# Fused attention and spatial gating on one core: fetches issued behind the last reader, separate buffers for the values' two readings, and a fixed start for the value parts

## The chip, the cores and the metric

The kernel runs on one core of a Trainium2 chip. The metric is the device time of one execution in microseconds (us). Two kernels are compared by the medians of their runs on the same chip. The profile is one execution, recorded by the hardware profiler; its times run from the first instruction.

## The reference

Attention in which neighbouring queries are averaged in twos, over 8 batches and 8 heads of 64, with 1152 keys and 576 pooled queries; its output goes through a gated unit with a spatial matrix over the 576 rows.

```python
def _attn_ref(q, k, v):                       # (8, 8, 1152, 64) each
    q_pool = q.reshape(B, H, S // 2, 2, D).mean(axis=3)
    scores = np.matmul(q_pool, k.transpose(0, 1, 3, 2)) / np.sqrt(D)
    scores = scores - np.max(scores, axis=-1, keepdims=True)
    attn = np.exp(scores)
    attn = attn / (np.sum(attn, axis=-1, keepdims=True) + 1e-09)
    return np.matmul(attn, v)

def _moe_ref(x, w_in, w_spatial, b_spatial, w_out):   # x: (8, 576, 512)
    h = np.maximum(x @ w_in, 0.0)
    u, v = h[..., :512], h[..., 512:]
    v_n = (v - v.mean(-1)) / np.sqrt(v.var(-1) + 1e-06)
    v_s = np.einsum('ts,bsd->btd', w_spatial, v_n) + b_spatial[None, :, None]
    return (u * v_s) @ w_out
```

## The kernel before

Numbers are float32, and matmuls take float16: each operand is scaled and split into a leading float16 part and a rest, and two or three products of parts stand for one product. The work is divided into 32 **pairs** (a batch and two heads); pair i belongs to batch i // 4. Four tasks belong to a pair, and each is a Python generator that issues a few instructions and then yields:

- `load_kq` (L218) fetches K and Q of a pair into one buffer `kq` (a single one for all pairs) in two transfers, L222 and L223, of 576 KB each. `prep` (L273) reads it: ScalarE squares of K and Q for a scale (L132 through L283, into a scratch part of `klo`), the sum over partitions on TensorE (L112) and the scale's exponent on VectorE (L117 to L122, `qkh`, `qks`, `qkr`), then the float16 parts: `xq` (L135), `qhi` (L138), scaled K (L302), its leading part `khi` (L304), its rest `klo` on GpSimd (L305), and nine copies between partitions, from L299 to L313, on the SyncE queue. Pair i + 2 is prepared while pair i is computed; there are three sets of these buffers.
- `norm_v` (L238) fetches the values of a pair (`load_v`, L226, 576 KB at L229 into `vt`, which has two buffers that the two tasks below take in turn) and squares them for the scale of the whole batch (L132 through L247). It runs four pairs ahead of the attention, because the scale of a batch needs its four pairs.
- `split_v` (L253) fetches the same values again and makes the leading part (L261, L262, on ScalarE) and the rest (L264, on GpSimd) in `vp`, one pair ahead.
- `maxima` (L317): 27 products with 384 keys on TensorE (L342, L333), each reduced on VectorE (L348), for the row maxima of the next pair; at its end they go as two rows into `xq` by a transfer (L363).

`attention` (L498) runs 18 steps of 128 keys for a pair: the scores' products (L506, L507) into one of three PSUM banks, the exponential on ScalarE (L512), a GpSimd subtraction that splits two tiles of probabilities (L524), and, four steps later, the values' products (L428, L432, L435). The generator yields 40 times, and at every such tick each of the pair's tasks is advanced at its own rate by `Pace` (L781): `Pace(gen, rate, at)` makes the first step when (ticks - at) x rate reaches 1. `values_ahead` (L267) chains norm_v of pair i + 4 and split_v of pair i + 1 at one rate of 0.35.

In pairs 0 to 7 the weights are converted from float64 (`load_weights`, L166) beside the attention, mostly on VectorE. After eight pairs a **gated unit** of two batches runs through the following eight, half a step per tick; the last one runs by itself at the end.

The order in which the engines do all this is not the order of the code. The framework schedules the recorded program: an instruction that is ready by its own estimate of times may be placed ahead of one that stands earlier in the code; the code's order counts as priority among those that are ready. Each engine then keeps the order that it was given, and waits in it.

Of the kernel before, what the change touches and what calls it, by code (L numbers as in the profile page):

```python
# [12 lines left out]
F32 = mybir.dt.float32  # L13
# [18 lines left out]
def attn_sgu_kernel(ctx: ExitStack, tc: tile.TileContext, qT, kT, v, w_in, w_spT, b_sp, w_out, out):  # L32
    nc = tc.nc
    P = 128
# [188 lines left out]
        nc.sync.dma_start(out=kq[:, KEYS:], in_=qT[b, hp].rearrange("h d r s -> (h d) (r s)"))  # L223
        state[i] = {"kq": kq}

    def load_v(i):  # L226
        b, hp = divmod(i, NHP)
        vt = ld.tile([P, 2, NC, D], F32, name="vt", bufs=2)
        nc.sync.dma_start(  # L229
            out=vt.rearrange("p h c d -> p h (c d)"),  # L230
            in_=v[b, 2 * hp : 2 * hp + 2].rearrange("h (p c) d -> p h (c d)", c=NC),
        )
        return vt

    vsq = {}
    vscale = {}

    def norm_v(i):  # L238

        b, hp = divmod(i, NHP)  # L240
        if hp == 0:
            vsq[b] = sm.tile([P, 2 * NHP], F32, name="vsq", bufs=2)
        vt = load_v(i)
        yield
        yield
        for h in range(2):
            square_sum(vsq[b][:, 2 * hp + h : 2 * hp + h + 1], vt[:, h], vt[:, h])  # L247
            yield
        if hp == NHP - 1:
            vscale[b] = yield from scale_of(vsq.pop(b), "v")  # L250
            yield

    def split_v(i):  # L253

        vt = load_v(i)
        yield
        yield
        s_v = vscale[i // NHP][0]
        vp = vps[i % 2]
        for h in range(2):  # L260
            nc.scalar.activation(vt[:, h], vt[:, h], AF.Copy, bias=0.0, scale=s_v)  # L261
            nc.scalar.activation(vp[:, h, :, D : 2 * D], vt[:, h], AF.Copy, bias=0.0, scale=1.0)  # L262
            yield
            nc.gpsimd.tensor_sub(vp[:, h, :, 0:D], vt[:, h], vp[:, h, :, D : 2 * D])  # L264
            yield

    def values_ahead(i):  # L267
        if i + NHP < NP:
            yield from norm_v(i + NHP)
        if i + 1 < NP:  # L270
            yield from split_v(i + 1)

    def prep(i):  # L273
        st = state[i]
        kq = st["kq"]
        X, KL, khh, qhl = (x[i % NSET] for x in (xq, klo, khi, qhi))
        k0 = kq[:, 0:KEYS].rearrange("p (c k) -> p c k", k=P)
        q0, q1 = kq[:, KEYS : KEYS + S], kq[:, KEYS + S :]
        st.update(qhl=qhl, khh=khh, X=X, KL=KL)

        sq = sm.tile([P, 2], F32, name="sq", bufs=2)
        for j in range(2):
            square_sum(sq[:, j : j + 1], kq[:, j * KEYS : (j + 1) * KEYS], KL[:, 0].rearrange("p c k -> p (c k)"))  # L283
            yield
        s, r = yield from scales(sq, "qk")
        esc = sm.tile([P, 1], F32, name="esc", bufs=NSET)
        nc.vector.scalar_tensor_tensor(
            out=esc, in0=r[:, 0:1], scalar=ESC, in1=r[:, 1:2], op0=ALU.mult, op1=ALU.mult
        )
        st["esc"] = esc  # L290
        s_k, s_q = s[:, 0:1], s[:, 1:2]
        nc.gpsimd.tensor_add(q0, q0, q1)
        yield

        lower, upper = slice(0, D), slice(D, P)
        head(X[:, 0], q0, s_q)
        rest(qhl[:, 1], q0, s_q, X[:, 0])
        yield
        nc.sync.dma_start(out=qhl[lower, 0], in_=X[lower, 0])  # L299
        nc.sync.dma_start(out=qhl[upper, 0], in_=qhl[lower, 1])  # L300
        for a, z in ((0, 5), (5, NC)):
            nc.scalar.activation(k0[:, a:z], k0[:, a:z], AF.Copy, bias=0.0, scale=s_k)  # L302
            yield
            nc.scalar.activation(khh[:, 1, a:z], k0[:, a:z], AF.Copy, bias=0.0, scale=1.0)  # L304
            nc.gpsimd.tensor_sub(KL[:, 0, a:z], k0[:, a:z], khh[:, 1, a:z])  # L305
            yield
        nc.sync.dma_start(out=khh[lower, 0], in_=khh[lower, 1])
        nc.sync.dma_start(out=khh[upper, 0], in_=khh[lower, 1])
        nc.sync.dma_start(out=qhl[lower, 1], in_=X[upper, 0])
        nc.sync.dma_start(out=khh[lower, 1], in_=khh[upper, 1])  # L310
        nc.sync.dma_start(out=X[lower, 1], in_=X[upper, 0])
        nc.sync.dma_start(out=KL[lower, 1], in_=KL[upper, 0])
        nc.sync.dma_start(out=KL[D:KR, 0], in_=KL[D:KR, 1])  # L313
        yield


# [54 lines left out]
    LAG = 4  # L371
    TAIL_SPLIT = 5
    TAIL_AT = 9
    PREP_AT = 3
    PREP_RATE = 0.35
    V_RATE = 0.35
    W_RATE = 0.25
    W_AT = 4
    MAX_RATE = 1.0
# [415 lines left out]
            gen = step(gen)  # L795

    load_kq(0)
    drain(norm_v(0))
    drain(prep(0))
    load_kq(1)  # L800
    for i in range(1, NHP):
        drain(norm_v(i))
    drain(maxima(0))
    drain(split_v(0))
    drain(prep(1))
# [1 line left out]
    spatial_weights = [None]  # L807
    credit = 0.0
    for i in range(NP):
        if i + 2 < NP:  # L810
            load_kq(i + 2)
        run = [
            Pace(maxima(i + 1), MAX_RATE) if i + 1 < NP else None,
            Pace(values_ahead(i), V_RATE),
            Pace(prep(i + 2), PREP_RATE, PREP_AT) if i + 2 < NP else None,
            Pace(weights, W_RATE, W_AT if i == 0 else 0),
        ]
        for _ in attention(i):
# [4 lines left out]
            while credit >= 1 and units:  # L823
                credit -= 1
                unit_step()
        for r in run[:3]:
            if r:
                drain(r.gen)
        weights = run[3].gen
        if ends_unit(i) and i < 2 * NHP:  # L830
            drain(weights)
            weights = None
# [50 lines left out]
```

## Time and profile before

| what | us |
| --- | --- |
| median of 3 runs (lowest, highest) | 1373.02 (1371.06, 1377.21) |
| profiled execution | 1378.83 |
| its span, first to last instruction | 1377.1 |
| first exponential (pair 0 begins) | 48.5 |
| pairs 0 to 7, with the weights' conversion | 280.1 |
| pair 31 and the last gated unit | 140.4 |
| TensorE / VectorE / ScalarE / GpSimd busy | 1222.1 / 967.1 / 970.6 / 847.0 |

In the rows of the profile PE is TensorE, PEld its weight load, DVE VectorE, ACT ScalarE, POOL GpSimd and SPq the queue of SyncE, which issues all transfers here. A row of a timeline has start, duration, engine, line, operation, out<-in; in brackets stands the idle time of the engine before it and what ended it. A row of waits has total, count and longest. A busy PE is not PE at its peak: matmuls are pipelined, and their ends are modelled.

### The profile page before, as it was taken

The numbers are of one execution on the slowest core, as the hardware profiler recorded it, in microseconds if no ns is written. First come the engines' busy times: TensorE is split into PE (matmuls) and PEld (weight loads), VectorE is DVE, ScalarE is ACT, GpSimd is POOL, SyncE is SP. The second block draws the span as 40 slices with busy tenths as digits, with TensorE's granted clock in tenths as the row PEclk, the third lists the DMA queues.
The fourth block names the chain that finished last, engine by engine and source line by source line (L and its number), as shares of the span: only waits on it lengthen the run. The fifth ranks groups of instructions, "written<-read, shape, count | busy, mean of one in ns | idle before, by whom it ended". The sixth has DMA issues, their size and how long they took to land.

```text
span 1377.1 us, 33478 instructions
## 1 busy us (share of the span) xinstructions
PE 1222.1 (89%) x13696; PEld 741.5 (54%) x13696; DVE 967.1 (70%) x2068; ACT 970.6 (70%) x1632; POOL 847.0 (62%) x492
## 2 busy tenths in 40 slices
PE   3677887788998999889998999889998999899998
PEld 1354555555554665556555666555555566556443
DVE  5799889986869767765668766775667866761455
ACT  6777678779966777768776886768776776655333
POOL 3587677878755666657774766667666576655000
PEclk9998899989999999999999999999999999999999
DMA  7533343434333231244332132244331131101002
GB/s 252 166 97 109 94 124 94 128 93 139 113 96 96 79 94 56 62 126 135 96 96 87 51 91 84 74 118 135 104 96 42 47 94 55 28 24 40 8 1 69
DMA packets 56346, 123.77 MB, mean 90 GB/s; under 512 B 8256, under 2 KB 16448, under 8 KB 56192
## 3 DMA queue, kind: packets, MB, share of 16 engines
q1 hardware_dynamic: 56192, 121.63, 29.8%
q8 instruction: 107, 1.75, 0.5%
q14 instruction: 47, 0.39, 0.1%
HBM read 83.56 MB, written 9.44 MB: 68 GB/s over the span
## 4 chain that ended last, share of the span: by engine, by line
PE 47%; DVE 25%; ACT 8%; POOL 7%; DMA 7%; issue 4%; SPq 1%; POOLq 0%; ACTq 0%; DVEq 0%
DVE mt L348 7%; PE pss L507 5%; PE pss L506 5%; PE pw L688 5%; POOL pt L524 4%; PE pm L342 4%; PE pw L731 4%; PE pw L646 3%; PE o L435 3%; PE o L428 3%; PE pw L582 3%; ACT pt L512 3%; DMA kq<-in_qT_dram 3%; PE o L432 3%; DVE vv L138 2%
## 5 line engine op out<-in xcount | busy, mean ns | idle before, releaser
L524 POOL TENSOR_TENSOR pt<-pt 128x1024 f16<-128x1024 f32 x288 | 567.8, 1977 | 265.9 <-ACT pt L512 253.8
L512 ACT ACTIVATE pt<-pss,lnp,esc 128x512 f32<-128x512 f32 x576 | 439.4, 776 | 156.7 <-PE pss L507 148.1
L348 DVE TENSOR_REDUCE mt<-pm 128x1 f32<-128x384 f32 x730 | 395.8, 552 | 139.1 <-PE pm L342 119.2
L435 PE MATMUL o<-vp,pt 128*128 128x65 f16 x2304 | 282.8, 198 | 20.2 <-POOL pt L524 19.9
L428 PE MATMUL o<-vp,pt 128*128 128x65 f16 x2304 | 284.8, 196 | 13.0 <-DVE xm L443 12.8
L506 PE MATMUL pss<-qhi,khi 128*128 128x64 f16 (+1 forms) x1152 | 279.6, 294 | 9.1 <-ACT pt L512 8.0
L432 PE MATMUL o<-vp,pt 128*128 128x64 f16 x2304 | 284.5, 196 | 0.0
L507 PE MATMUL pss<-xq,klo 66*128 66x64 f16 (+1 forms) x1152 | 280.6, 295 | 4.1 <-DMA xq<-mr 4.1
L428 PEld LDWEIGHTS <-pt 128*128 128x128 bf16 x2304 | 222.7, 101 | 85.1 <-DVE xm L443 22.0
L432 PEld LDWEIGHTS <-pt 128*128 128x128 bf16 x2304 | 221.6, 100 | 50.7 <-issue 10.5
L342 PE MATMUL pm<-khi,qhi 128*128 128x384 f16 x652 | 217.9, 335 | 32.6 <-DVE mt L348 27.7
L435 PEld LDWEIGHTS <-pt 128*128 128x128 f16 x2304 | 220.7, 100 | 31.6 <-POOL pt L524 24.8
L507 PEld LDWEIGHTS <-klo 66*128 66x128 f16 x1152 | 99.1, 100 | 48.8 <-issue 17.3
L132 ACT ACTIVATE klo<-kq 128x1152 f16<-128x1152 f32 x64 | 74.6, 1166 | 63.7 <-DMA kq<-in_kT_dram 49.4
L506 PEld LDWEIGHTS <-khi 128*128 128x128 f16 x1152 | 103.5, 100 | 27.9 <-issue 12.2
L342 PEld LDWEIGHTS <-qhi 128*128 128x128 f16 x768 | 76.8, 101 | 66.3 <-issue 28.5
L524 POOL TENSOR_TENSOR ptl<-ptl 128x1152 f16<-128x1152 f32 x32 | 71.1, 2221 | 57.9 <-ACT ptl L520 57.9
L305 POOL TENSOR_TENSOR klo<-kq,khi 128x640 f16<-128x640 f32 x64 | 85.1, 1341 | 20.1 <-ACT khi L304 19.8
L520 ACT ACTIVATE ptl<-pss,lnp,esc 128x256 f32<-128x256 f32 (+1 forms) x128 | 75.6, 591 | 24.8 <-PE pss L507 24.2
L264 POOL TENSOR_TENSOR vp<-vt,vp 128x576 f16<-128x576 f32 x64 | 80.6, 1264 | 20.3 <-ACT vp L262 20.3
L582 PE MATMUL pw<-wi_h,xg 128*128 128x512 f16 x240 | 90.1, 382 | 0.0
L731 PE MATMUL pw<-wo_h,vv 128*128 128x512 f16 x216 | 80.3, 381 | 4.7 <-DVE vv L138 4.7
(177 smaller groups left out, 2394.2 us busy)
## 6 DMA issues: line engine op xcount, KB each, us to landing
vt<-in_v_dram SPq DMA_DIRECT2D x64, 576.0 KB
kq<-in_kT_dram SPq DMA_DIRECT2D x32, 576.0 KB
kq<-in_qT_dram SPq DMA_DIRECT2D x32, 576.0 KB
khi<-khi SPq DMA_DIRECT2D x96, 144.0 KB
out_dram<-row SPq DMA_DIRECT2D x24, 256.0 KB
qhi<-xq SPq DMA_DIRECT2D x64, 72.0 KB
klo<-klo SPq DMA_DIRECT2D x32, 144.0 KB
vv<-in_w_in_dram SPq DMA_DIRECT2D x8, 512.0 KB
```

The source lines that it names most:

```text
L305: nc.gpsimd.tensor_sub(KL[:, 0, a:z], k0[:, a:z], khh[:, 1, a:z])
L342: nc.tensor.matmul(pm[:, :W], lhsT=qhl[:, h, c0 : c0 + P], rhs=khh[:, h, n * NB : (n + 1) * NB, :], start=True, stop=True,)
L348: nc.vector.reduce_max(out=mt[:, t, n : n + 1], in_=pm[:, :W], axis=AX.X)
L428: nc.tensor.matmul(o[:, t], lhsT=top[:, cols], rhs=vp[:, D : D + D1], start=c == 0 and t == 0, stop=False, skip_group_check=True,)
L432: nc.tensor.matmul(o[:, t, 0:D], lhsT=top[:, cols], rhs=vp[:, 0:D], start=False, stop=False, skip_group_check=True)
L435: nc.tensor.matmul(o[:, t], lhsT=rst[:, cols], rhs=vp[:, D : D + D1], start=False, stop=c == NC - 1, skip_group_check=True,)
L506: nc.tensor.matmul(o, lhsT=khh[:, h, c, :], rhs=qhl[:, h, q], start=True, stop=False)
L507: nc.tensor.matmul(o, lhsT=KL[0:KR, h, c, :], rhs=X[0:KR, h, q], start=False, stop=True)
L512: nc.scalar.activation(pt, ps, AF.Exp, bias=lnp, scale=esc)
L524: nc.gpsimd.tensor_sub(t.bitcast(F16)[:, :, 0::2], t, t.bitcast(BF16)[:, :, 1::2])
L582: nc.tensor.matmul(ph, lhsT=xa[:, cc, c0 : c0 + P], rhs=wa[:, cc, DH:DF], start=n == 0, stop=n == 3 * NCC - 1,)
L731: nc.tensor.matmul(py, lhsT=ga[:, fc, c0 : c0 + P], rhs=wa[:, fc, :], start=m == 0, stop=m == end - 1)
```

## The change

1. **K and Q**: `load_kq(i + 1)` is called at the end of `prep(i)`, behind the last copy, and no longer at the beginning of a pair's loop pass. PREP_AT goes from 3 to 2.
2. **Values**: the one name `vt` with two buffers becomes two names, `vn` for the squares and `vs` for the parts, with one buffer each; the fetch into a buffer is issued at the end of the task that has read it, for the next pair (`load_v(i + ahead, name)`).
3. **Rates**: norm_v and split_v are paced apart, norm_v at 0.4 from tick 0, split_v at 0.3 from tick 16 on.
4. **The start**: the squares of pairs 0 and 2 go through `vn`, those of 1 and 3 through `vs`, and the preparation of pair 0 stands ahead of the squares in the code.

The arithmetic is the same.

```diff
@@ -223,38 +223,40 @@
         nc.sync.dma_start(out=kq[:, KEYS:], in_=qT[b, hp].rearrange("h d r s -> (h d) (r s)"))
         state[i] = {"kq": kq}
 
-    def load_v(i):
-        b, hp = divmod(i, NHP)
-        vt = ld.tile([P, 2, NC, D], F32, name="vt", bufs=2)
-        nc.sync.dma_start(
-            out=vt.rearrange("p h c d -> p h (c d)"),
-            in_=v[b, 2 * hp : 2 * hp + 2].rearrange("h (p c) d -> p h (c d)", c=NC),
-        )
-        return vt
+    vts = {}
+
+    def load_v(i, name):
+
+        if i < NP:
+            b, hp = divmod(i, NHP)
+            vt = ld.tile([P, 2, NC, D], F32, name=name)
+            nc.sync.dma_start(
+                out=vt.rearrange("p h c d -> p h (c d)"),
+                in_=v[b, 2 * hp : 2 * hp + 2].rearrange("h (p c) d -> p h (c d)", c=NC),
+            )
+            vts[i, name] = vt
 
     vsq = {}
     vscale = {}
 
-    def norm_v(i):
+    def norm_v(i, name="vn", ahead=1):
 
         b, hp = divmod(i, NHP)
         if hp == 0:
             vsq[b] = sm.tile([P, 2 * NHP], F32, name="vsq", bufs=2)
-        vt = load_v(i)
-        yield
-        yield
+        vt = vts.pop((i, name))
         for h in range(2):
             square_sum(vsq[b][:, 2 * hp + h : 2 * hp + h + 1], vt[:, h], vt[:, h])
             yield
+        load_v(i + ahead, name)
+        yield
         if hp == NHP - 1:
             vscale[b] = yield from scale_of(vsq.pop(b), "v")
             yield
 
     def split_v(i):
 
-        vt = load_v(i)
-        yield
-        yield
+        vt = vts.pop((i, "vs"))
         s_v = vscale[i // NHP][0]
         vp = vps[i % 2]
         for h in range(2):
@@ -263,12 +265,8 @@
             yield
             nc.gpsimd.tensor_sub(vp[:, h, :, 0:D], vt[:, h], vp[:, h, :, D : 2 * D])
             yield
-
-    def values_ahead(i):
-        if i + NHP < NP:
-            yield from norm_v(i + NHP)
-        if i + 1 < NP:
-            yield from split_v(i + 1)
+        load_v(i + 1, "vs")
+        yield
 
     def prep(i):
         st = state[i]
@@ -311,6 +309,8 @@
         nc.sync.dma_start(out=X[lower, 1], in_=X[upper, 0])
         nc.sync.dma_start(out=KL[lower, 1], in_=KL[upper, 0])
         nc.sync.dma_start(out=KL[D:KR, 0], in_=KL[D:KR, 1])
+        if i + 1 < NP:
+            load_kq(i + 1)
         yield
 
 
@@ -371,9 +371,11 @@
     LAG = 4
     TAIL_SPLIT = 5
     TAIL_AT = 9
-    PREP_AT = 3
+    PREP_AT = 2
     PREP_RATE = 0.35
-    V_RATE = 0.35
+    NORM_RATE = 0.4
+    V_RATE = 0.3
+    V_AT = 16
     W_RATE = 0.25
     W_AT = 4
     MAX_RATE = 1.0
@@ -795,11 +797,13 @@
             gen = step(gen)
 
     load_kq(0)
-    drain(norm_v(0))
+    load_v(0, "vn")
+    load_v(1, "vs")
     drain(prep(0))
-    load_kq(1)
-    for i in range(1, NHP):
-        drain(norm_v(i))
+    drain(norm_v(0, "vn", 2))
+    drain(norm_v(1, "vs", 2))
+    drain(norm_v(2, "vn", 2))
+    drain(norm_v(3, "vs", -3))
     drain(maxima(0))
     drain(split_v(0))
     drain(prep(1))
@@ -807,11 +811,11 @@
     spatial_weights = [None]
     credit = 0.0
     for i in range(NP):
-        if i + 2 < NP:
-            load_kq(i + 2)
         run = [
             Pace(maxima(i + 1), MAX_RATE) if i + 1 < NP else None,
-            Pace(values_ahead(i), V_RATE),
+            Pace(norm_v(i + NHP), NORM_RATE) if i + NHP < NP else None,
+
+            Pace(split_v(i + 1), V_RATE, V_AT) if i + 1 < NP else None,
             Pace(prep(i + 2), PREP_RATE, PREP_AT) if i + 2 < NP else None,
             Pace(weights, W_RATE, W_AT if i == 0 else 0),
         ]
@@ -823,10 +827,10 @@
             while credit >= 1 and units:
                 credit -= 1
                 unit_step()
-        for r in run[:3]:
+        for r in run[:4]:
             if r:
                 drain(r.gen)
-        weights = run[3].gen
+        weights = run[4].gen
         if ends_unit(i) and i < 2 * NHP:
             drain(weights)
             weights = None
```

What the scheduler makes of this is seen in the orders. Line numbers of the changed kernel are lower by 2 in `prep` (L305 was L307, L310 was L312, L302 was L304), higher by 2 in `split_v` (L263 was L261) and from the attention on (L514 was L512, L522 was L520), and L229 has become L233.

**First place**: SyncE's queue, around the fetch of K and Q for pair 20, during pair 17. Before:

```order
L307 DMA khi_117<-khi_117 64x1152
L308 DMA khi_117<-khi_117 64x1152
L309 DMA qhi_120<-xq_114 64x576
L312 DMA klo_108<-klo_108 64x1152
L222 DMA kq<-in_kT_dram 128x1152
L310 DMA khi_117<-khi_117 64x1152
L313 DMA klo_108<-klo_108 2x1152
L223 DMA kq<-in_qT_dram 128x1152
L229 DMA vt<-in_v_dram 128x2x576
```

After:

```order
L305 DMA khi_117<-khi_117 64x1152
L306 DMA khi_117<-khi_117 64x1152
L310 DMA klo_108<-klo_108 64x1152
L222 DMA kq<-in_kT_dram 128x1152
L308 DMA khi_117<-khi_117 64x1152
L311 DMA klo_108<-klo_108 2x1152
L223 DMA kq<-in_qT_dram 128x1152
L363 DMA xq_113<-mr 1x9x128 x2
L233 DMA vs<-in_v_dram 128x2x576
```

K's fetch stands directly behind the copy of `klo` in both; the values' fetch has moved behind the row of the maxima.

**Second place**: ScalarE at the start, up to the first exponential (`pt`). `xq`, `kq` and `khi` belong to the preparation of pair 1, `vp_102` to the values of pair 1, `u` and `vv` to the weights. Before:

```order
L261 ACTIVATE vt<-vt,vs 128x576 x2
L262 ACTIVATE vp_102<-vt 128x9x64 x2
L135 ACTIVATE xq_114<-kq,qks 128x576
L302 ACTIVATE kq<-kq,qks 128x640
L302 ACTIVATE kq<-kq,qks 128x512
L304 ACTIVATE khi_117<-kq 128x640
L304 ACTIVATE khi_117<-kq 128x512
L132 ACTIVATE vv,wiq<-u 128x512
L150 ACTIVATE u<-vv 128x512
L132 ACTIVATE vt,vsq<-vt 128x576 x2
L157 ACTIVATE vv<-vv,bias_e 128x512
L512 ACTIVATE pt<-pss,lnp,esc 128x512 x2
```

After:

```order
L150 ACTIVATE u<-vv 128x512
L135 ACTIVATE xq_114<-kq,qks 128x576
L300 ACTIVATE kq<-kq,qks 128x640
L300 ACTIVATE kq<-kq,qks 128x512
L302 ACTIVATE khi_117<-kq 128x640
L302 ACTIVATE khi_117<-kq 128x512
L263 ACTIVATE vs<-vs 128x576 x2
L264 ACTIVATE vp_102<-vs 128x9x64 x2
L157 ACTIVATE vv<-vv,bias_e 128x512
L514 ACTIVATE pt<-pss,lnp,esc 128x512 x2
```

The split of pair 1's values has moved behind the preparation, and the weights' steps L132 and L150 and two squares have moved ahead of it.

**Third place**: ScalarE between the last exponentials of pair 11 and the first of pair 12; `vsq` marks the squares of values, `ptl` the exponentials of the last 64 queries. Before:

```order
L512 ACTIVATE pt<-pss,lnp,esc 128x512 x2
L261 ACTIVATE vt<-vt,vs 128x576
L512 ACTIVATE pt<-pss,lnp,esc 128x512
L261 ACTIVATE vt<-vt,vs 128x576
L512 ACTIVATE pt<-pss,lnp,esc 128x512
L520 ACTIVATE ptl<-pss,lnp,esc 128x5x64
L512 ACTIVATE pt<-pss,lnp,esc 128x512
L520 ACTIVATE ptl<-pss,lnp,esc 128x5x64
L512 ACTIVATE pt<-pss,lnp,esc 128x512
L132 ACTIVATE row,gsq<-u 128x576
```

After:

```order
L132 ACTIVATE vn,vsq<-vn 128x576
L514 ACTIVATE pt<-pss,lnp,esc 128x512
L132 ACTIVATE vn,vsq<-vn 128x576
L514 ACTIVATE pt<-pss,lnp,esc 128x512 x3
L132 ACTIVATE vn,vsq<-vn 128x576 x2
L522 ACTIVATE ptl<-pss,lnp,esc 128x5x64
L514 ACTIVATE pt<-pss,lnp,esc 128x512
L522 ACTIVATE ptl<-pss,lnp,esc 128x5x64
L132 ACTIVATE vn,vsq<-vn 128x576
L132 ACTIVATE row,gsq<-u 128x576
```

Two pairs' squares and the first half of a third's stand here now where none stood before, and a fetch of 576 KB lies between one pair's and the next's.

## The prediction

> **What bounds the kernel now.** I read the page's totals first, then the view by stages, then single pairs of heads side by side, then the waits.
>
> ```profile
> span 1377.1 us, 33478 instructions
> PE 1222.1 (89%) x13696; PEld 741.5 (54%) x13696; DVE 967.1 (70%) x2068; ACT 970.6 (70%) x1632; POOL 847.0 (62%) x492
> ...
> 0.00:48.50 48.50, 16.31 (x51) 5.90 (x52) 27.96 (x65) 30.95 (x62) 17.12 (x22) 1.00 0.71 226
> 48.50:328.60 280.10, 224.58 (x2803) 147.37 (x2803) 246.49 (x457) 215.70 (x364) 214.55 (x118) 0.90 0.37 109
> ```
>
> The columns of a stage are its length, then busy time of PE, PE's weight load, DVE, ACT and POOL, then the granted clock. Over the whole span PE is 89% busy. The start, 48.5 us until the first exponential, is a chain of fetches and small steps (PE 16.3 us busy). In the next 280.1 us, while the weights are converted, DVE is the fullest (246.5 of 280.1, PE 224.6). After that come the steady pairs:
>
> ```profile
> 405.00:451.30 46.30, 40.27 (x432) 24.26 (x430) 41.49 (x89) 31.95 (x55) 25.91 (x15) 0.93 0.25 74
> 451.30:490.00 38.70, 36.55 (x439) 23.05 (x438) 23.78 (x54) 30.62 (x53) 26.95 (x17) 1.00 0.29 86
> 490.00:530.10 40.10, 39.32 (x476) 24.29 (x474) 28.12 (x64) 28.98 (x51) 25.44 (x15) 1.00 0.29 83
> 530.10:568.60 38.50, 36.99 (x463) 22.59 (x461) 27.72 (x64) 26.91 (x48) 27.07 (x16) 1.00 0.30 86
> ...
> 845.70:885.00 39.30, 37.04 (x463) 22.61 (x461) 27.71 (x64) 26.82 (x47) 27.00 (x16) 1.00 0.28 84
> ...
> 1160.10:1199.30 39.20, 36.76 (x463) 22.44 (x461) 29.49 (x63) 23.54 (x39) 26.50 (x15) 1.00 0.11 25
> ```
>
> These are pairs 10 to 13, 21 and 29. In most of them PE is busy for 94 to 98% (39.32 of 40.10 in pair 12); pair 10, in which the gated unit normalises, is DVE's (41.49 of 46.30). ACT has about 10 us to spare in each.
>
> **The K and Q fetch.** What ACT waits for:
>
> ```profile
> ACT klo L132 <- DMA kq<-in_kT_dram: 49.4, 20, 4.7
> ACT klo L132 <- DMA kq<-in_qT_dram: 8.8, 12, 1.9
> ...
> 704.25 0.46 SPq L312 DMA_DIRECT2D klo<-klo  x1
> 704.77 0.88 SPq L222 DMA_DIRECT2D kq<-in_kT_dram  x1
> ...
> 707.93 0.38 SPq L223 DMA_DIRECT2D kq<-in_qT_dram  x1
> ...
> 710.01 1.16 ACT L132 ACTIVATE klo<-kq 128x1152 f16<-128x1152 f32 x1 [3.97 <-DMA kq<-in_kT_dram]
> ```
>
> ACT stands 49.4 + 8.8 = 58.2 us for these fetches. But the issue at 704.77 already comes 0.52 us after the L312 copy, which waits for the last reader of the buffer (the subtraction L305): the scheduler has hoisted it out of the next loop pass. The first order shown above has the same rows around it in the changed kernel: L222 directly behind the klo copy, then two copies, then L223. So **this edit gains 0 us**: the fetch is issued where it was. What hides the wait is PE's own work: pair 29 prepares no further pair and fetches no K, and takes 39.20 us against 39.30 of pair 21, which does. If that cover fails, the price is the one wait of PE at the end of that path:
>
> ```profile
> PE o L435 <- POOL pt L524: 19.9, 24, 2.3
> ```
>
> That is 19.9 us in the whole span, so I bound this edit by -10 (half of it gone) and +4. The +4: behind the last cast of a pair and ahead of the next K square 27 fewer short ACT operations stand now, over the last 21 pairs, so ACT waits 27 x 0.67 = 18 us longer there; a fifth of such waits reaching PE would be 4 us. PREP_AT moves the first step by one tick and is inside these bounds.
>
> **The start.** Now one buffer takes the values of pairs 1 and 3 for the squares and of pairs 0 and 1 for the splits in turn, so two fetches that stood one behind the other are serial with their readers.
>
> ```profile
> 29.22 0.37 SPq L229 DMA_DIRECT2D vt<-in_v_dram  x1
> ...
> 33.21 0.68 ACT L132 ACTIVATE vt<-vt 128x576 f32<-128x576 f32 x1 [0.17 <-DMA vt<-in_v_dram]
> ...
> 39.12 1.44 ACT L261 ACTIVATE vt<-vt,vs 128x576 f32<-128x576 f32 x2 [4.46 <-DMA vt<-in_v_dram]
> ...
> 39.62 0.15 DVE L122 TENSOR_SCALAR qkr<-qkh 128x2 int32<-128x2 int32 x1
> ...
> 41.21 2.43 POOL L264 TENSOR_TENSOR vp<-vt,vp 128x576 f16<-128x576 f32 x2 [6.23 <-ACT vp L262]
> ...
> 41.61 0.76 ACT L135 ACTIVATE xq<-kq,qks 128x576 f16<-128x576 f32 x1
> ...
> 43.30 1.06 PE L507 MATMUL pss<-xq,klo 66*128 66x512 f16 x3 [4.09 <-DMA xq<-mr]
> ...
> 44.75 0.61 ACT L132 ACTIVATE vv<-u 128x512 f32<-128x512 f32 x1
> ...
> 47.83 0.72 ACT L157 ACTIVATE vv<-vv,bias_e 128x512 int32<-128x512 int32 x1 [0.52 <-DVE vv L155]
> 48.46 1.43 ACT L512 ACTIVATE pt<-pss,lnp,esc 128x512 f32<-128x512 f32 x2
> ```
>
> A free fetch of values takes 33.21 - 29.22 = 4.0 us. Before, ACT stands until 39.12 for the values of split 1, splits them (2.5 us, to 41.61), prepares pair 1 (3.1 us, to 44.75), then does the weights' steps until 48.46. After, the second order above has the preparation ahead of split 1. Step by step: the squares of pair 3 still end near 29.1, the fetch for split 0 lands at 33.2, its parts end on POOL 43.64 - 39.12 = 4.5 us later, at 37.7; the fetch for split 1 lands at 37.9 + 4.0 = 41.9. Meanwhile the scales are there at 39.8, the preparation runs to 42.9, split 1 to 45.4, L157 takes 0.6, and the first exponential starts at 46.0 instead of 48.5: **-2.4 us**. The ends: not before its product (43.30 + 1.06 = 44.4, so -4.1); if the fetch meets other transfers and takes 6.8 us, as the one from 20.93 to 27.76 did, -0.6 at 47.9.
>
> ```profile
> 20.93 6.80 DMA vt<-in_v_dram
> ```
>
> **The squares of the values.** With a buffer of their own, their fetch waits only for squares, so the scheduler draws them forward: the 12 pairs of squares that stood beside pairs 14 to 25 now stand, with the four that belong there, between pair 9.9 and pair 13.6 (third order above). Costs:
>
> ```profile
> 641.55 0.69 ACT L132 ACTIVATE vt<-vt 128x576 f32<-128x576 f32 x1
> ...
> 642.89 0.78 ACT L512 ACTIVATE pt<-pss,lnp,esc 128x512 f32<-128x512 f32 x1
> 643.02 0.38 SPq L229 DMA_DIRECT2D vt<-in_v_dram  x1
> ...
> 647.00 1.44 ACT L261 ACTIVATE vt<-vt,vs 128x576 f32<-128x576 f32 x2 [0.36 <-DMA vt<-in_v_dram]
> ...
> 722.30:768.70 46.40, 40.69 (x432) 24.23 (x430) 41.14 (x89) 31.73 (x55) 25.07 (x14) 0.93 0.24 72
> ...
> 1038.20:1083.40 45.20, 38.84 (x432) 23.25 (x431) 41.47 (x89) 30.41 (x51) 24.93 (x14) 0.96 0.21 60
> ```
>
> Two squares take 642.89 - 641.55 = 1.34 us, so 12 x 1.34 = 16.1 us of ACT move into pairs 10 to 13. A new wait comes on top. A fetch lands 647.00 - 643.02 = 4.0 us after its issue, which the release precedes by some 0.4: 4.4 us. In the new order ten of these sixteen have only 1.2 to 3.6 us of ACT work since the squares before (three exponentials and nothing else in one case); the shortfalls add up to 18.4 us. Behind the waiting square on ACT stand the exponentials, and PE waits for those; on SP the row of the maxima (L363) and the copies of the next preparation stand behind a fetch that waits for its buffer. ACT was busy for 31.95 + 30.62 + 28.98 + 26.91 = 118.5 of 163.6 us there and waited some 8 us for K and Q, which leaves 37 us for 34.5 of new demand: it just fits, with nothing over. One direct comparison prices it: pair 18 (with one pair of squares) took 46.40, pair 26 (none, and else the same unit's step) 45.20, so 1.2 us in a normalising pair; elsewhere, where PE has no slack to lose, I take 0.1, the difference between pairs 21 and 29. 2.5 more in pair 10 and 9.5 in the others give 3 + 1 = **+4 us**; ends 0 (all in ACT's idle time) and +16 (34.5 less half of the 37, if half of the idle time lies where neither falls). Later the twelve are gone: 1.2 + 11 x 0.1 = **-2.3 us** (0 to -3.5).
>
> By the Trainium skill's page "SBUF — State Buffer", section "Summary: rules for kernel authors", such a fetch would be estimated with 358 GB/s, about 1.6 us for 576 KB; the row above shows 4.0, and the measurement decides. By the page the shortfalls would all but vanish and the +4 with them, and the sum would be near 1368.
>
> **The weights' stage.** There DVE's order changes (maxima of pairs 6 and 7 now stand ahead of the previous pair's divisions), with the same operations. Term 0. DVE idles 280.1 - 246.5 = 33.6 us there; a third of that either way, 11 us, is the bound.
>
> ```profile
> 8.99 0.16 DVE L287 SCALAR_TENSOR_TENSOR esc<-qkr 128x1 f32<-128x1 f32 x1
> ...
> L287 DVE SCALAR_TENSOR_TENSOR esc<-qkr 128x1 f32<-128x1 f32 x8 | 10.6, 1329 | 0.0
> ```
>
> A one-column DVE operation takes 0.16 us with POOL idle and 1.33 in this stage, so small shifts against POOL move DVE's time both ways. The same section of that page says that a DVE operation with two SBUF inputs and a GpSimd operation block each other fully; this row agrees, though it alone doesn't show the partner.
>
> **Sum.** -2.4 + 0 + 4 - 2.3 + 0 = -0.7 us against the profiled execution (span 1377.1, 1378.83 in all, so 1378.1). That execution lay 5.8 us above the median of the runs, 1373.02; on the runs' scale the forecast is **1372 us**.
>
> **Rivals.**
> 1. The fetch waits do go (the hoist differs on the chip): half of PE's 19.9 us, with the start, 1373 - 10 - 2.4 = about 1361. For it: 58.2 us of waits. Against: same rows in the order, and pair 29. Chance 0.08.
> 2. The weights' stage gains: 1373 - 11 - 1 = about 1361. For it: 33.6 us of DVE idle time and a new order; against: the operations are the same. Chance 0.20.
> 3. **Slower**: ACT becomes the bound in pairs 10 to 13. The waits there overlap no idle time of ACT, because that lies in other places. It decides once the waits and squares exceed 37 us, that is once a fetch takes over 4.6 us instead of 4.4 (ten fetches, 2.5 us left). Then 1373 - 2.4 - 2.3 + 16 = about 1384, and 1388 with the +4 of the K and Q fetch. Chance 0.22.
> 4. The edit doesn't do what it says: for K and Q that is my forecast.
>
> **How the numbers follow.** The forecast, within 0.5% (6.9 us, about what can be told from no change), has 0.46; the other 0.04 are split. Faster 0.08 + 0.20 + 0.02 = 0.30, same 0.46, slower 0.22 + 0.02 = 0.24. The range reaches from somewhat below rivals 1 and 2 to rival 3: 1358 to 1388.
>
> **What would show it.** In the changed profile: first exponential at 46 us (44.4 to 47.9); ACT's wait for K and Q still near 58 us, or more; a new wait of ACT squares for values' fetches, near 18 us, in pairs 10 to 13, and those pairs 4 us longer in sum; pairs 14 to 25 shorter by 2. If the K and Q wait falls below 30 us, or the weights' stage differs from 280 us by over 5, the prediction is wrong in that step.

## The result, and the profile after

The changed kernel takes 1410.88 us (median of 4 runs, 1407.43 to 1412.98) beside 1372.04 for the kernel before on the same chip: a ratio of 1.0275, 95% interval 1.0237 to 1.0313. It is 39 us slower by the medians. The forecast was 1372, its range 1358 to 1388. The profiled execution took 1412.54.

The totals of the changed kernel's page:

```profile
span 1410.8 us, 33474 instructions
PE 1231.4 (87%) x13696; PEld 745.1 (53%) x13696; DVE 983.3 (70%) x2068; ACT 972.4 (69%) x1632; POOL 851.0 (60%) x492
```

The same numbers of instructions keep DVE busy 16 us longer (967.1 before). Next the view by stages of the changed kernel: start, weights' stage, pairs 10 to 13, 18 to 25, 26 to 30, and pair 29 alone (columns as in the prediction):

```profile
0.00:47.40 47.40, 16.45 (x51) 5.80 (x52) 27.99 (x65) 31.09 (x62) 16.19 (x21) 1.00 0.72 230
47.40:320.00 272.60, 219.35 (x2787) 143.43 (x2787) 241.16 (x453) 215.79 (x361) 218.70 (x120) 0.92 0.37 113
...
401.80:578.50 176.70, 155.00 (x1786) 94.36 (x1784) 125.99 (x268) 132.11 (x251) 104.60 (x61) 0.97 0.37 112
...
731.90:1057.80 325.90, 297.87 (x3424) 182.56 (x3423) 223.56 (x486) 223.81 (x357) 209.20 (x121) 0.98 0.26 74
1057.80:1270.50 212.70, 190.56 (x2182) 116.69 (x2181) 153.74 (x322) 135.09 (x219) 125.38 (x71) 0.96 0.17 49
...
1190.50:1233.80 43.30, 38.68 (x463) 23.39 (x461) 31.68 (x63) 24.71 (x41) 26.95 (x15) 0.96 0.14 36
```

The three steady stages in the kernel before:

```profile
405.00:568.60 163.60, 153.13 (x1806) 94.19 (x1803) 121.11 (x269) 118.46 (x204) 105.36 (x61) 0.98 0.28 82
...
722.30:1038.20 315.90, 295.42 (x3424) 181.11 (x3422) 217.53 (x487) 233.35 (x389) 208.33 (x121) 0.98 0.31 92
1038.20:1236.70 198.50, 184.75 (x2182) 113.18 (x2180) 149.29 (x322) 134.24 (x218) 125.43 (x71) 0.98 0.17 49
```

The start gained 1.1 us and the weights' stage 7.5. Pairs 10 to 13 lost 13.1, 18 to 25 lost 10.0, 26 to 30 lost 14.2; with pairs 8 and 9 (81.8, before 76.4), pairs 8 to 30 lose 42 in all. Pair 29 reads no values for squares and fetches no K, and still goes from 39.2 to 43.3. The last square of values ends in pair 13 of the changed kernel. So something other than the value squares costs in pairs 18 to 30, where a gated unit runs beside the attention.

ScalarE's waits for fetches in the changed kernel (total, count, longest):

```profile
ACT klo L132 <- DMA kq<-in_kT_dram: 45.5, 17, 4.0
ACT klo L132 <- DMA kq<-in_qT_dram: 8.5, 9, 2.3
ACT vn L132 <- DMA vn<-in_v_dram: 7.9, 8, 1.8
```

K and Q: 54.0 us, near the 58.2 of before, as forecast. The squares' new wait is 7.9 us, not 18.

**Pair 29.** A piece of the changed kernel's timeline; `qhi` is the rest of Q, `u` the gated unit's product, `mt` a maximum:

```profile
1204.88 0.75 DVE L697 SCALAR_TENSOR_TENSOR row<-pw,r_v,b_bc 128x512 f32<-128x512 f32 x1
...
1205.55 1.16 DVE L138 SCALAR_TENSOR_TENSOR qhi<-kq,qks,xq 128x576 f16<-128x576 f32 x1
1206.05 2.41 POOL L526 TENSOR_TENSOR pt<-pt 128x1024 f16<-128x1024 f32 x1
...
1206.63 2.38 DVE L700 TENSOR_TENSOR u<-u,row 128x512 f32<-128x512 f32 x1
...
1208.93 0.54 DVE L348 TENSOR_REDUCE mt<-pm 128x1 f32<-128x384 f32 x1
...
1209.53 0.32 PE L342 MATMUL pm<-khi,qhi 128*128 128x384 f16 x1 [2.05 <-DVE mt L348]
```

The same place before:

```profile
1172.22 0.81 DVE L138 SCALAR_TENSOR_TENSOR qhi<-kq,qks,xq 128x576 f16<-128x576 f32 x1
...
1174.85 0.74 DVE L695 SCALAR_TENSOR_TENSOR row<-pw,r_v,b_bc 128x512 f32<-128x512 f32 x1
...
1175.50 0.55 DVE L348 TENSOR_REDUCE mt<-pm 128x1 f32<-128x384 f32 x1
1175.97 1.43 DVE L698 TENSOR_TENSOR u<-u,row 128x512 f32<-128x512 f32 x1
```

Before, the rest of Q is done ahead of the row, and a maximum stands between row and product. After, the rest of Q has slid between row and product, the product meets a GpSimd subtraction and ends only 0.55 us behind it (1209.01, 1208.46), and the maximum comes 4 us after the row. TensorE waits 2.05 us for it. An engine that is 70% busy on average sets the pace here, because beside a gated unit the program gives TensorE only two banks for the maxima.

### The profile page after: what moved, and what is told of

Its sections match the earlier page's. It is cut to its first block, busy times and chain, and to the rows that moved or that the text cites. A ratio compares the mean times of both kernels' runs of the same rounds, so it can differ in the third digit from the quotient of the medians.

```text
span 1410.8 us, 33474 instructions
## 1 busy us (share of the span) xinstructions
PE 1231.4 (87%) x13696; PEld 745.1 (53%) x13696; DVE 983.3 (70%) x2068; ACT 972.4 (69%) x1632; POOL 851.0 (60%) x492
## 4 chain that ended last, share of the span: by engine, by line
PE 42%; DVE 27%; ACT 9%; POOL 8%; DMA 7%; issue 5%; SPq 1%; POOLq 0%; DVEq 0%; ACTq 0%
DVE mt L348 8%; PE pss L508 5%; PE pss L509 5%; POOL pt L526 5%; PE pm L342 4%; PE pw L690 4%; PE pw L733 4%; PE pw L648 3%; ACT pt L514 3%; PE pw L584 3%; DMA kq<-in_kT_dram 3%; PE o L437 3%; PE o L430 2%; PE o L434 2%; DVE vv L138 2%
## 5 line engine op out<-in xcount | busy, mean ns | idle before, releaser
L514 ACT ACTIVATE pt<-pss,lnp,esc 128x512 f32<-128x512 f32 x576 | 440.9, 777 | 184.3 <-PE pss L509 180.0
L430 PE MATMUL o<-vp,pt 128*128 128x65 f16 x2304 | 285.5, 197 | 19.8 <-DVE xm L445 19.6
L508 PE MATMUL pss<-qhi,khi 128*128 128x64 f16 (+1 forms) x1152 | 280.1, 295 | 8.5 <-ACT pt L514 7.8
L437 PEld LDWEIGHTS <-pt 128*128 128x128 f16 x2304 | 221.3, 100 | 21.0 <-POOL pt L526 14.2
L132 ACT ACTIVATE klo<-kq 128x1152 f16<-128x1152 f32 x64 | 74.5, 1164 | 60.9 <-DMA kq<-in_kT_dram 45.5
L266 POOL TENSOR_TENSOR vp<-vs,vp 128x576 f16<-128x576 f32 x64 | 85.4, 1335 | 16.7 <-ACT vp L264 16.6
L522 ACT ACTIVATE ptl<-pss,lnp,esc 128x256 f32<-128x256 f32 (+1 forms) x128 | 75.6, 590 | 22.8 <-PE pss L509 22.5
L290 POOL TENSOR_TENSOR kq<-kq 128x576 f32<-128x576 f32 x32 | 47.2, 1476 | 72.9 <-ACT klo L132 58.8
```

The costliest lines, as they stand in the source:

```text
L430: nc.tensor.matmul(o[:, t], lhsT=top[:, cols], rhs=vp[:, D : D + D1], start=c == 0 and t == 0, stop=False, skip_group_check=True,)
L437: nc.tensor.matmul(o[:, t], lhsT=rst[:, cols], rhs=vp[:, D : D + D1], start=False, stop=c == NC - 1, skip_group_check=True,)
L508: nc.tensor.matmul(o, lhsT=khh[:, h, c, :], rhs=qhl[:, h, q], start=True, stop=False)
L514: nc.scalar.activation(pt, ps, AF.Exp, bias=lnp, scale=esc)
```

## The experiments

Each changed part was run alone and in pairs, then one cause after another was taken out. Ratios are to the kernel before on the same chip, with 95% intervals; a stage's time comes from one profile. Executions of one kernel differ by up to 14 us (run 14: 1354.35 to 1368.38). Pair 29, 39.2 or 39.1 in the kernel before and in runs 2, 3, 4 and 8, repeats to 0.1 us.

### Which part costs: runs 1 to 4

**Run 1**, on the kernel before:

```diff
-    PREP_AT = 3
+    PREP_AT = 2
```

> The kernel before with PREP_AT 2 in place of 3 and nothing else. Theory A (the preparation one tick earlier changes VectorE's order: one maximum fewer stands ahead of the scale steps, and the leading part of Q falls behind the gated unit's row and beside a GpSimd subtraction, so the maxima come late and PE waits): about +42 us over the 23 pairs from pair 8 to 30 and no gain at the start, 1400 to 1420 us. Theory B (the values: bunched squares and one buffer for each reading): no change, 1372 +- 5. Theory C (the place of the K and Q fetch): no change, 1372 +- 5.

Measured: 1390.11 us, 1.0132 (1.0092 to 1.0171). Theory A holds in kind but not in size: pairs 8 to 30 lost 25.6 us (pair 29: 43.1), and pairs 0 to 7 gained 13.2 (266.9).

**Run 2**, on the changed kernel:

```diff
-    PREP_AT = 2
+    PREP_AT = 3
-        if i + 1 < NP:
-            load_kq(i + 1)
...
     for i in range(NP):
+        if i + 2 < NP:
+            load_kq(i + 2)
```

> The changed kernel without its first part: PREP_AT 3 and the K and Q fetch at the beginning of a loop pass, but the values' two buffers, their rates, V_AT 16 and the new start. Theory A: the loss is gone and the start's 1 us and the weights' stage's 7 us stay, 1360 to 1372 us. Theory B: the loss stays, 1405 to 1415. Theory C: the loss is gone as under A.

Measured: 1387.89 us, 1.0124 (1.0071 to 1.0176). Theory A alone falls. Pairs 10 to 13 take 174.6 (before 163.6), the other steady stages are within 3 us, and pair 29 is at 39.2. The values cost too, at another place.

**Run 3**, the K and Q lines of the change alone on the kernel before:

```diff
+        if i + 1 < NP:
+            load_kq(i + 1)
...
-        if i + 2 < NP:
-            load_kq(i + 2)
```

> The kernel before with the K and Q fetch issued at the end of the preparation, PREP_AT 3. Theory A and B, and the prediction: 0 us, 1368 to 1376, with ScalarE's wait for K and Q still near 58 us. Theory C: 1405 to 1415.

Measured: 1373.58 us, 0.9999 (0.9980 to 1.0018). Nothing, as forecast; ScalarE's wait for K and Q is 61.9 us.

**Run 4**, the changed kernel with `PREP_AT = 3`:

> The changed kernel with PREP_AT 3 in place of 2. Theory A: the 42 us are gone, 1360 to 1372 us, and the leading part of Q stands ahead of the gated unit's row again in pair 29. Theory B: 1405 to 1415. Theory C: 1405 to 1415.

Measured: 1384.03 us, 1.0072 (1.0051 to 1.0094): the rest of Q stands ahead of the row again and pair 29 takes 39.2, but pairs 10 to 13 take 174.1. So there are two causes: PREP_AT, and the values.

### What the early step does: runs 5, 6, 13, 15, 16 and 17

**Run 5**, on run 1's kernel; `hold` is 4, the steps up to the scales, the next one follows at once, and all later steps of the preparation come one step sooner too:

```diff
                 self.gen = step(self.gen)
+                self.n += 1
+                if self.n == self.hold:
+                    self.sum += 1.0
```

> The kernel before with PREP_AT 2, as in the first run, and Q's leading part and rest taken one step (2.9 ticks) sooner behind the scales, so that in pairs 13, 21 and 29 VectorE's rest of Q (L138) stands ahead of the gated unit's row again, while the scales stay as early as in the first run. Theory A1 (that rest, behind the row, puts the unit's product against a GpSimd subtraction and the maxima come late): pairs 13, 21 and 29 go back to within 1 us of 38.5, 39.3 and 39.2 (from 41.7, 40.4 and 43.1), and the whole falls from 1390 to about 1380. Theory A2 (the scales themselves, one maximum earlier, and TensorE's sum for them): those pairs and the whole stay, 1390 +- 5.

Measured: 1394.49 us, 1.0156 (1.0124 to 1.0189). Pairs 13, 21 and 29 took 39.1, 39.2 and 39.5: the place of these steps, and not of the scales, is what cost there, as A1 has it. The whole did not fall: pairs 8 to 30 lost 14.9 instead of 25.6, but the weights' stage took 279.7 instead of 266.9.

**Run 6**, on the kernel before:

```diff
-            Pace(prep(i + 2), PREP_RATE, PREP_AT) if i + 2 < NP else None,
+            Pace(prep(i + 2), PREP_RATE, 2 if i < 2 * NHP else PREP_AT) if i + 2 < NP else None,
```

> The kernel before with PREP_AT 2 in pairs 0 to 7 and 3 behind them. In the first run pairs 0 to 7 took 266.9 us instead of 280.1, and pairs 8 to 30 lost 26. If both are the step's own doing, this has the gain without the loss: about 1361 us. Rival: pairs 0 to 7 differ between kernels by chance of their order (276.0 in the third run, whose edit has no work there), so that 1365 to 1375 comes out.

Measured: 1365.99 us, 0.9948 (0.9929 to 0.9967). Pairs 0 to 7 took 268.7, and pairs 8 to 30 are within 2 us of before. So the early step costs where a gated unit runs. That it pays elsewhere isn't shown: the rival (pairs 0 to 7 differ by chance of their order) expected 1365 to 1375 and holds as well. In the profiles of this study pairs 0 to 7 took 266.9 to 287.6 us with the early step there and 265.8 to 280.1 without it.

**Run 13**, on run 1's kernel: the row stays in PSUM, so the product reads one operand from there. The arithmetic is the same.

```diff
-                    out=gg[:, :n], in0=pz[:, :n], scalar=r_v, in1=b_bc[:, ba : ba + n], op0=ALU.mult, op1=ALU.add
+                    out=pz[:, :n], in0=pz[:, :n], scalar=r_v, in1=b_bc[:, ba : ba + n], op0=ALU.mult, op1=ALU.add
                 )
-                nc.vector.tensor_mul(u[:, fc, a : a + n], u[:, fc, a : a + n], gg[:, :n])
+                nc.vector.tensor_mul(u[:, fc, a : a + n], u[:, fc, a : a + n], pz[:, :n])
```

> The first run's kernel (PREP_AT 2 alone), and the gated unit's product takes its second operand, the row, from PSUM, where the row is written in place. Theory A1 (the product is held up by GpSimd while it reads two operands from SBUF): it takes 0.7 us whether GpSimd works or not, pairs 13, 21 and 29 go from 41.7, 40.4 and 43.1 to within 1 us of 38.5, 39.3 and 39.2, and the whole from 1390 to about 1378. Theory A3 (the order of the maxima behind Q's rest is the loss, whatever the product takes): those pairs stay within 1 us of the first run's.

Measured: 1379.77 us, 1.0068 (1.0042 to 1.0093). The product in the view of lines, by shape (busy, mean in ns), in the changed kernel:

```profile
L700 DVE TENSOR_TENSOR u<-u,row 128x512 f32<-128x512 f32 x32 | 33.6, 1051 | 0.4
```

In the kernel before, and in run 13:

```profile
L698 DVE TENSOR_TENSOR u<-u,row 128x512 f32<-128x512 f32 x32 | 27.5, 858 | 0.4
```

```profile
L698 DVE TENSOR_TENSOR u<-u,pw 128x512 f32<-128x512 f32 x27 | 18.3, 678 | 0.0
```

And run 13's pair 29 by stage and at the place shown above:

```profile
1164.90:1202.30 37.40, 37.00 (x466) 22.79 (x464) 26.50 (x63) 23.46 (x39) 23.53 (x15) 1.00 0.11 26
```

```profile
1180.59 0.81 DVE L698 TENSOR_TENSOR u<-u,pw 128x512 f32<-128x512 f32 x2
1180.81 1.90 POOL L524 TENSOR_TENSOR pt<-pt 128x1024 f16<-128x1024 f32 x1
...
1181.32 1.02 DVE L348 TENSOR_REDUCE mt<-pm 128x1 f32<-128x384 f32 x2
...
1182.25 1.07 DVE L138 SCALAR_TENSOR_TENSOR qhi<-kq,qks,xq 128x576 f16<-128x576 f32 x1
```

A GpSimd subtraction starts in the middle of the products, and they don't notice: no 128x512 product takes over 0.68 us. Pairs 13, 21 and 29 take 39.2, 38.4 and 37.4. That is what A1 expects, but it doesn't rule out A3: in this kernel the rest of Q has moved on behind the product and two maxima, so the maxima are no longer behind it either. The rows of pair 29 above favour A1. The product takes 2.38 - 0.68 = 1.70 us longer there than a free one and the rest of Q 1.16 - 0.81 = 0.35 longer than before, together the 2.05 us of the wait; this is an estimate from these rows. The Trainium skill's page "SBUF — State Buffer", section "Who interferes with whom", says that a VectorE instruction with two SBUF inputs contends with a GpSimd instruction that reads SBUF, and that one with at most one such input, outside its 2-port modes, does not; the rows of the product agree.

**Runs 15 and 16**, the same edit on the kernel before and on the changed kernel:

> The kernel before with the product's operand from PSUM and nothing else. Collisions hidden in the old order: 1368 to 1376, pairs 13, 21 and 29 within 0.5 us. Collisions that cost even there: 1360 to 1367.

> The changed kernel with the product's operand from PSUM. Theory A1: pairs 13, 21 and 29 (44.1, 44.1 and 43.3) lose 3 to 4 us each and the whole comes to about 1395; theory A3: 1408 to 1414.

Measured: run 15 1365.50 us, 0.9957 (0.9941 to 0.9973), pair 29 36.6; run 16 1394.21 us, 1.0175 (1.0160 to 1.0190), pairs 13, 21 and 29 39.4, 38.6 and 37.5. The product's collisions cost some 6 us even in the old order, and 14 (by the ratios) to 17 (by the medians) in the changed kernel. So they make only 8 to 10 of the 39 us between the two kernels. With the product in PSUM on both sides, run 16 is still 2.2% slower than run 15, and its pairs 8 to 30 take 939.0 us beside 898.1, a loss about as large as the 42 us with the row in SBUF. Pairs 18, 26 and 27 even take longer than in the changed kernel (51.8, 51.6 and 45.3 beside 48.9, 49.8 and 42.0).

**Run 17**. What run 13 left lay in the pairs in which the unit normalises. TensorE's waits in pair 26 of the changed kernel:

```profile
PE o L430 <- DVE xm L445: 3.6, 1, 3.6
PE pm L112 <- DVE mt L348: 2.8, 1, 2.8
PE pm L342 <- DVE mt L348: 2.8, 3, 1.4
```

And of the kernel before:

```profile
PE pm L342 <- DVE mt L348: 4.0, 3, 2.2
PE o L428 <- DVE xm L443: 1.0, 1, 1.0
```

The preparation's sum (L112) stood behind a maximum for 2.8 us, and the values' products behind a division of VectorE (`xm`) for 3.6 us. On run 13's kernel:

```diff
-            Pace(prep(i + 2), PREP_RATE, PREP_AT) if i + 2 < NP else None,
+            Pace(prep(i + 2), PREP_RATE, 3 if i >= 8 and i % 8 == 2 else PREP_AT) if i + 2 < NP else None,
```

> The thirteenth run's kernel (PREP_AT 2, product from PSUM) with PREP_AT 3 in pairs 10, 18 and 26. If the early step is what costs there (its sum over partitions and its scales stand between the normalisation's steps on TensorE and VectorE): those pairs go from 50.4, 50.1 and 48.9 to within 1 us of 46.3, 46.4 and 45.2, and the whole from 1379.8 to 1366 to 1371. If it is a neighbour's doing (what the pair before leaves behind): less than half of the 11.5 us goes.

Measured: 1371.69 us, 0.9980 (0.9958 to 1.0002). Pairs 10, 18 and 26 took 46.7, 45.2 and 45.2: what they had lost was the step's doing. In pair 26 the two waits, 2.8 and 3.7 us in run 13, fall to 0.3 and 1.0. The rest of the early step's price stays open: beside run 15, which has the same product and the old step, pairs 8 to 30 of this run are still 12 us longer (910.2 beside 898.1, the most in pair 17, 41.1 beside 37.5), and what costs there was not tried.

### What the values cost: runs 7 and 8

A piece of run 2's timeline, in pair 13:

```profile
530.17 0.61 ACT L520 ACTIVATE ptl<-pss,lnp,esc 128x320 f32<-128x320 f32 x1
533.42 0.68 ACT L132 ACTIVATE vn<-vn 128x576 f32<-128x576 f32 x1 [2.64 <-DMA vn<-in_v_dram]
...
534.11 0.76 ACT L512 ACTIVATE pt<-pss,lnp,esc 128x512 f32<-128x512 f32 x1
```

And in pair 27, where ScalarE waits for the single buffer of the parts:

```profile
1115.84 0.77 ACT L263 ACTIVATE vs<-vs 128x576 f32<-128x576 f32 x1 [3.11 <-DMA vs<-in_v_dram]
...
1117.58 0.77 ACT L512 ACTIVATE pt<-pss,lnp,esc 128x512 f32<-128x512 f32 x1
```

In both places a fetch holds up the exponential that stands behind it on ScalarE (in pair 27 with two short steps of the gated unit in between).

**Run 7**, on run 2's kernel (pair 4's first fetch also stands behind the start's squares, to keep the turns):

```diff
-            vt = ld.tile([P, 2, NC, D], F32, name=name)
+            vt = ld.tile([P, 2, NC, D], F32, name="vt", bufs=2)
```

> The second run's kernel (values' part alone) with the two buffers shared in turn again (one name with two buffers), fetches still issued at the end of a task: squares of the values stand beside the pairs where they stood before, not drawn forward. Theory B1 (the loss of 11 us in pairs 10 to 13 is the squares drawn forward into them): pairs 10 to 13 go back to 163.6 +- 2 us from 174.6, the whole to 1370 to 1377. Theory B2 (the loss is the split held back to tick 16, or the rates): pairs 10 to 13 stay near 174, the whole near 1388.

Measured: 1382.25 us, 1.0073 (1.0047 to 1.0099). Pairs 10 to 13 are back at 165.5, as B1 has it, but the whole is not: the last pairs of the batches, 15, 19, 23 and 27, took 2.6, 2.7, 3.6 and 3.7 us more than before. There the parts belong to the next batch, and they are held back to tick 16 in this run too. That this is what costs there was not tried by itself.

**Run 8**, on run 2's kernel:

```diff
-            vt = ld.tile([P, 2, NC, D], F32, name=name)
+            vt = ld.tile([P, 2, NC, D], F32, name=name, bufs=2 if name == "vn" else 1)
```

> The second run's kernel with two buffers for the squares' values, so that ScalarE hardly waits for their fetch while the squares stay drawn forward (30 of 56 late ones into pairs 9 to 12). If the loss in pairs 10 to 13 is the wait for the fetch: those pairs go back to 163.6 +- 3. If it is the squares' own time on ScalarE and what they push back: they stay at 171 to 176 or go over, and the whole stays near 1388.

Measured: 1368.96 us, 0.9980 (0.9963 to 0.9998). ScalarE's wait for the squares fell from 10.2 to 1.0 us, and pairs 10 to 13 took 166.0. Seven of their squares moved on to pairs 8 and 9; over pairs 8 to 13, with nearly as many squares as in run 2 (36 beside 38, 14 before), 3.6 us of a loss of 10.1 are left. So most of it was the wait, and little the squares' own time. Of the 19 us between runs 2 and 8, some 10 came from the weights' stage (265.8).

### Both mended, and the best version: runs 9 to 12, 14 and 18

**Runs 9 to 12** put the edits of runs 6 and 8 into the changed kernel (9), into run 2's (10), and each alone into the changed kernel (run 6's: 11, run 8's: 12).

> The changed kernel with two mends: PREP_AT 2 only in pairs 0 to 7 and 3 behind them, and two buffers for the squares' values. If the loss is the step in the pairs with a gated unit plus ScalarE's wait for the values' fetch, nothing of the 38 us is left, and the gains of the sixth and eighth run (start 43.5, pairs 0 to 7 near 266 us) come on top: 1355 to 1366 us. If something else of the change costs time (the K and Q fetch beside the two, the split held back to tick 16), 1372 to 1385.

> As the ninth run, but with the K and Q fetch at the beginning of a loop pass as before. If the K and Q edit is worth nothing, as the third run showed beside the kernel before, this comes out within 0.4% of the ninth run; if it costs or gains something in company with the others, the two differ by more.

> The changed kernel with PREP_AT 2 only in pairs 0 to 7, one buffer for the squares as in the change. By theory A the 27 us between the changed kernel and the fourth run lie in pairs 8 to 30 and go: 1376 to 1386, with pairs 10 to 13 still near 174 us. By theory B, that the one buffer is most of it, over 1395.

> The changed kernel with two buffers for the squares' values and PREP_AT 2 throughout. If the wait for that fetch costs 9 to 11 us in pairs 10 to 13 beside the early step too, and up to 10 more come from the weights' stage as between the second and the eighth run: 1390 to 1402, with pairs 18 to 30 as long as in the changed kernel (538.5 us). If the two losses are one and the same stall: 1408 to 1414.

Measured:

| run | us | ratio (95%) | weights' stage | pairs 10-13 | pairs 18-30 |
| --- | --- | --- | --- | --- | --- |
| changed | 1410.88 | 1.0275 (1.0237, 1.0313) | 272.6 | 176.7 | 538.6 |
| 9 | 1390.61 | 1.0131 (1.0112, 1.0149) | 285.5 | 165.9 | 521.1 |
| 10 | 1375.95 | 1.0023 (1.0006, 1.0041) | 271.8 | 168.2 | 522.3 |
| 11 | 1378.82 | 1.0052 (1.0029, 1.0075) | 268.0 | 167.9 | 520.8 |
| 12 | 1417.34 | 1.0325 (1.0303, 1.0346) | 287.6 | 170.5 | 538.7 |

Runs 9 and 12 lie outside every range that was expected of their totals, and run 10 differs from run 9 by 1.1% instead of 0.4. In the steady stages PREP_AT out of the later pairs takes nearly 18 us off pairs 18 to 30, as expected; the second buffer takes 9 (run 8 against 2), 6 (run 12 against the change) and only 2 us (run 9 against 11) off pairs 10 to 13. Run 11 keeps the single buffer and still has 167.9 in pairs 10 to 13, with 8.7 us of the wait in them: how much of a wait reaches TensorE depends on where it falls. What broke the totals is the weights' stage: run 9 is 13.7 us longer there than run 10, from which it differs by the K and Q lines alone. The stage in run 8, the shortest, and in run 12, the longest:

```profile
43.50:309.30 265.80, 211.50 (x2770) 138.73 (x2769) 235.73 (x459) 218.69 (x371) 216.79 (x119) 0.94 0.40 120
```

```profile
43.10:330.70 287.60, 226.86 (x2802) 147.46 (x2802) 256.26 (x463) 221.62 (x377) 217.16 (x120) 0.89 0.37 113
```

VectorE is busy 20.5 us longer with nearly the same instructions, and the stage is 21.8 us longer. In all twenty profiles of this study its length less VectorE's busy time lies between 28 and 36 us. So this stage is VectorE's, and its time follows how long VectorE's operations take. That the extra time lies beside GpSimd can be counted in the profiles: for each operation and shape take the median of those executions that no GpSimd instruction overlaps. What the overlapped executions of the stage take above it adds up to 58 us in run 8 and 77 in run 12, which is 18 of the 20.5 us. By the same count pairs 8 to 30 hold 82 us before and 102 after the change, 68 and 85 with the product in PSUM (runs 15 and 16): the product is one of several operations that are held up. How much of this reaches TensorE, and which lines bring it about, was not tried.

**Run 14**, the edits of runs 6 and 13 together on the kernel before, and **run 18**, the same two on the changed kernel:

> The sixth run's kernel (PREP_AT 2 in pairs 0 to 7, 3 behind them) with the product's operand from PSUM. If collisions of the product cost TensorE time in the pairs with a gated unit even in the old order: 4 to 10 us below the sixth run, 1356 to 1362. If they are hidden there (TensorE is 94 to 98% busy in those pairs): 1364 to 1368.

> The changed kernel with PREP_AT 2 only in pairs 0 to 7 and the product from PSUM: what is left of the change is the K and Q fetch and the values' part, to be set beside the fourteenth run (1359.6). If the values' part costs what the second run showed (14 us beside the kernel before), 1370 to 1377; if its cost was itself collisions of the product, 1356 to 1364.

Measured: run 14 1359.63 us, 0.9923 (0.9901 to 0.9945), the fastest of all and below both kernels; run 18 1375.17 us, 1.0011 (0.9992 to 1.0029). What lies between them, 0.9%, is the values' part with the K and Q lines, so most of the values' cost (1.2% in run 2) is not a collision of the product.

## Why the prediction was wrong

1. **The step that failed** is the sentence in the K and Q part: PREP_AT "moves the first step by one tick and is inside these bounds" (-10 to +4). It got no price of its own; the bounds were made from ScalarE's waits for the fetches and one wait of TensorE behind them. The prediction also took pair 29 for one that prepares no further pair, and so for a measure of what a preparation costs; but the rest of Q in the rows above is pair 31's, and pair 29 lacks only the fetch of a next K and Q and the squares of values. What the constant moves is the sum L112 on TensorE and the scales on VectorE, one maximum earlier, and behind them the rest of Q. Alone it costs 1.3% (run 1); out of the later pairs of the changed kernel it gives back 2.2% (run 11 against the change). Of the 25.6 us that run 1 lost in pairs 8 to 30, some 12 belong to the pairs that normalise (run 17 against run 13); a further part lies at the product in pairs 13, 21 and 29; 12 us are left open (run 17 against run 15). One part of the price stands in the prediction: it names operations that GpSimd holds up, with 0.16 and 1.33 us, but only for the weights' stage, with "small shifts". The pairs with a gated unit have such an operation too, in the chain that TensorE waits on.
2. **The value squares**: the mechanism was right, the size was not. The term +4 (0 to +16) measured +11.0 in pairs 10 to 13 with the values alone (run 2). The first half of rival 3 is what happened in this part, the waits overlap no idle time of ScalarE: run 8 takes the wait away, and the 11 us shrink to 2.4 (in pairs 8 to 13, 10.1 to 3.6). The condition it named, waits and squares above 37 us, did not hold: in these pairs of the changed kernel the wait was at most 7.9 us, and ScalarE was busy 13.7 us longer (132.1 beside 118.5). The waits were overestimated (18; 10.2 in run 2 and 7.9 in the changed kernel), and the share of them that reaches TensorE underestimated: the term took a tenth of a microsecond for a pair, from two pairs in which no square of the values waits. The 37 us of idle time answered how much ScalarE can do, not whether an exponential stands behind a wait.
3. **Later pairs 14 to 25**, -2.3: with the values alone 153.4 + 316.9 beside 153.7 + 315.9, so +0.7 (run 2). Their going gave nothing that can be seen.
4. **The start**, -2.4 (-0.6 to -4.1): the first exponential came at 47.4, -1.1.
5. **The weights' stage**, 0 within 11: 7.5 us shorter, inside the bound, but beyond the 5 us at which the prediction called this step wrong. Nearly the same operations took VectorE 5.3 us less (241.2 beside 246.5). The kernels of this study spread from 265.8 to 287.6, -14 to +8 of the kernel before.
6. **K and Q fetch**, 0: right beside the kernel before (run 3); beside the other edits it changes the weights' stage (runs 9 and 10).

The range ended at 1388, rival 3 with 4 us for the K and Q fetch. That run 2, the values alone, also comes to 1388 is luck, since its parts are others. The changed kernel is 27 us above run 4, which lacks the early step alone, and that step is what put it out of the range.

## What to carry to other kernels

A constant that moves one task by a tick is priced by the rows it changes on each engine in its order, and above all on those whose result a two-bank loop waits for. Where VectorE and GpSimd both work from SBUF, look for VectorE operations with two durations in the view of lines; an operand left in PSUM takes such an operation out of the collision (0.4% here). A wait moved to ScalarE is free only if no exponential stands behind it: count what is queued behind the wait, not the idle time of the engine.

## What the runs showed of the hardware

VectorE's 128x512 product with both operands in SBUF took 0.68 to 0.69 us free and up to 2.38 beside a GpSimd subtraction; with one operand in PSUM never more than 0.68. A one-input operation can be held up as well. In the changed kernel:

```profile
L121 DVE TENSOR_SCALAR qks<-qkh 128x2 int32<-128x2 int32 x32 | 17.9, 559 | 0.6
...
L121 DVE TENSOR_SCALAR vs<-vh 128x1 int32<-128x1 int32 x8 | 1.2, 152 | 0.2
```

The same line takes 559 ns on average with two columns (up to 2.08 us) and 152 with one (never over 0.16, though GpSimd works beside most of them). The maxima's reductions from PSUM take 0.52 to 0.56 us with and without GpSimd beside them. In pair 29 of the changed kernel the granted clock was 0.96, beside 1.00 before and in run 13, and TensorE was busy for 38.68 us beside 36.76 and 37.00; with the wait of 2.05 us that makes up nearly all of the 4.1 us that the pair lost. A wait need not bring the lower clock with it: pair 21 of run 1 had one of 2.04 us at a clock of 1.00 and lost 1.1.
